# Loads and casts at the start of a fused relu-squared attention and gated FFN kernel: the first keys, the first queries, the activation table and one cast

## The chip, the cores and the metric

The kernel runs on one core of a Trainium2 chip. The time is the device time of one execution in microseconds (us). The core has five engines with queues of their own: TensorE (PE) multiplies matrices, VectorE (DVE) and ScalarE (ACT) do elementwise work, GpSimd (POOL) here mostly issues loads, and SyncE (SP) issues transfers. Sixteen DMA engines move the data for all of them.

## The reference

```
scores = scale * q @ k^T                 # 8 batches, 12 heads, 448 x 448, head size 64
attn   = relu(scores)^2 / 448
x      = (attn @ v), heads side by side  # 3584 x 768
out    = (relu(x @ w_gate) * (x @ w_val)) @ w_out   # 768 -> 1536 -> 768
```

Inputs and output are float32. The kernel works in bfloat16 with float32 accumulation and folds all constant factors into the scale of the last copy.

## The kernel before, in words

The batches (b from 0 to 7) are worked one after the other. The attention of batch b is interleaved with the FFN of batch b - 1, so that TensorE has matmuls while the other engines do relu and square. Every instruction is pinned with `pin`: each engine executes its instructions in the order in which the program writes them. What the program orders by hand is thus the whole schedule.

**Loads.** A tensor q, k or v of one batch has 12 heads of 448 rows by 64. `load_nat` (L110) brings some heads of it with two loads: rows 0 to 255, four to a partition, into partitions 0 to 63 ("lo"), and rows 256 to 447, three to a partition, into partitions 64 to 127 ("hi"). The fourth place of the upper partitions stays zero for keys and queries; memsets at L81 put the zeros there, into the tiles kn and qn of both buffers. These loads go through Pool's queue (`dma_in`, L92) and turn float32 into bfloat16 on their way. Pool's queue carries, in this order (L334 to L346): q and k of batch 0, v, the first two column chunks of w_gate and w_val, k and q of batch 1, the third chunk, v of batch 1, the fourth chunk, w_out in two halves (wo0, wo1), and later the k, q and v of the next batches.

**The first two heads** take another way (`load_first`, L95, called with 2). They are loaded without a change of type by SP's and ACT's queues, keys ahead of queries, into the tiles kr and qr, which are used as float32 scratch here and which otherwise serve from batch 3 on. Then VectorE casts the keys into kn (L107) and ScalarE casts the queries into qn (L108). The load of ScalarE's activation table comes ahead of ScalarE's first activation, which is that cast. Pool clears the empty place in the scratch tiles (L101) and then makes the identity matrix (L89) from a tile that VectorE zeroes (L83); after that its loads begin, with heads 2 and 3, 4 to 7, and 8 to 11.

**The first batch** (`first_batch`, L380) has no FFN beside it. TensorE begins with 28 matmuls on zeros (`idle_matmuls`, 14 pairs). For each of the six pairs of heads it then transposes keys and queries by matmuls with the identity (`transposes`, L169), and VectorE copies the result to the tile kq_sb (L180). The score matmuls of a pair fill three tiles of PSUM (buffers: 3). ScalarE takes the relu of each tile (L185), VectorE the square (L189). There are 21 such tiles. Two to four pairs of idle matmuls stand between. At the end of the batch the value matmuls (`av_pair`, L224) come in between the last score tiles: `values(qd, c)` sums attn times v for two heads in one of two PSUM banks, and `cast` (L390) copies the sum to x in bfloat16, on VectorE except for one, values(2, 0), which ScalarE casts (L428). `low_values` (L123) moves a part of v on VectorE ahead of the first value matmuls.

**The FFN** of batch 0 follows at once. `gv_unit` (L258) does 128 of the 1536 hidden columns: 12 matmuls for the gate, a relu on ScalarE (L266), 12 for the value, a product on VectorE (L272). Eight such units run before batch 1 begins. `out_unit` (L284) multiplies the hidden tile by w_out: the first six of its twelve steps read wo0, the last six wo1, and between them other work may run (L292).

Of the kernel before, what the change touches and what calls it, by code (L numbers as in the profile page):

```python
# [9 lines left out]
FP32 = mybir.dt.float32  # L10
BF16 = mybir.dt.bfloat16
AF = mybir.ActivationFunctionType
# [4 lines left out]
def kernel(  # L17
# [15 lines left out]
    nc = tc.nc  # L33

    B, H, S, D = q.shape
    d_model, d_ff = moe_w_gate.shape
# [13 lines left out]
    const = ctx.enter_context(tc.tile_pool(name="const", bufs=1))  # L50
# [3 lines left out]
    rpool = ctx.enter_context(tc.tile_pool(name="rpool", bufs=4))  # L54
# [5 lines left out]
    def pin(ins):  # L60
        return tc.keep_in_program_order(ins)
# [10 lines left out]
    NB = 2  # L72
    blank = const.tile([128, S], BF16, name="blank")
    pin(nc.vector.memset(blank, 0.0))
    kn_b = [const.tile([128, H, 4, D], BF16, name=f"kn{i}") for i in range(NB)]
    qn_b = [const.tile([128, H, 4, D], BF16, name=f"qn{i}") for i in range(NB)]
    v_b = [const.tile([128, H, 4, D], BF16, name=f"vn{i}") for i in range(NB)]
    ident = const.tile([128, 128], BF16, name="ident")
    for n in range(NB):
        for t in (kn_b[n], qn_b[n]):  # L80
            pin(nc.vector.memset(t[64:128, :, 3, :], 0.0))  # L81
        if n == 0:
            pin(nc.vector.memset(ident, 0.0))  # L83

    kr = const.tile([128, 4, d_model], BF16, name="kr")
    qr = const.tile([128, 4, d_model], BF16, name="qr")

    def make_ident():
        pin(nc.gpsimd.affine_select(out=ident, in_=ident, compare_op=ALU.not_equal, fill=1.0, base=0,  # L89
                                    pattern=[[-1, 128]], channel_multiplier=1))  # L90

    def dma_in(o, i):  # L92
        pin(nc.gpsimd.dma_start(out=o, in_=i))  # L93

    def load_first(h1):  # L95

        staged = []
        for grp, src in ((kr, k), (qr, q)):
            st = grp.rearrange("p i m -> p (i m)")[:, 0:h1 * 8 * D].bitcast(FP32)
            st = st.rearrange("p (h i d) -> p h i d", i=4, d=D)  # L100
            pin(nc.gpsimd.memset(st[64:128, :, 3, :], 0.0))  # L101
            lo = src[0, 0:h1, 0:256, :].rearrange("h (j i) d -> j h i d", i=4)
            hi = src[0, 0:h1, 256:448, :].rearrange("h (j i) d -> j h i d", i=3)
            pin(nc.sync.dma_start(out=st[0:64], in_=lo))
            pin(nc.scalar.dma_start(out=st[64:128, :, 0:3, :], in_=hi))
            staged.append(st)
        pin(nc.vector.tensor_copy(kn_b[0][:, 0:h1], staged[0]))  # L107
        pin(nc.scalar.activation(qn_b[0][:, 0:h1], staged[1], AF.Copy))  # L108

    def load_nat(dst, src, b, h0, h1):  # L110
        lo = src[b, h0:h1, 0:256, :].rearrange("h (j i) d -> j h i d", i=4)
        hi = src[b, h0:h1, 256:448, :].rearrange("h (j i) d -> j h i d", i=3)
        dma_in(dst[0:64, h0:h1, :, :], lo)
        dma_in(dst[64:128, h0:h1, 0:3, :], hi)

    def load_qk(b, h0=0, h1=H):
        load_nat(kn_b[b % NB], k, b, h0, h1)
        load_nat(qn_b[b % NB], q, b, h0, h1)
# [4 lines left out]
    def low_values(b):  # L123

        t = v_b[b % NB].rearrange("p (q s h) i d -> p q s h i d", s=2, h=2)
        pin(nc.vector.tensor_copy(t[64:128, :, 1, :, 3, :], t[0:64, :, 1, :, 3, :]))
# [64 lines left out]
    def relu2(src, dst, n):  # L191
        square_part(dst, relu_part(src, n))
# [31 lines left out]
    def av_pair(b, qd, c, attn, ps):  # L224

        p = HALVES[c][1]
        for h2, o in HALVES:
            mm(ps[o, :S], v_b[b % NB][p, 4 * qd + 2 * c + h2, 3, :], attn[p, 6 + h2, :], True, False)
        for i in range(3):
            for h2, o in HALVES:  # L230
                mm(ps[o, :S], v_b[b % NB][:, 4 * qd + 2 * c + h2, i, :], attn[:, 8 * c + 2 * i + h2, :], False, i == 2)

    def bank_tile():
        return psum.tile([128, 512], FP32, name="xT_ps", tag="acc", bufs=2)

    def idle_matmuls(ps, n):

        for _ in range(n):
            mm2(ps[:, :S], blank[:, 0:128], blank, True, True)
# [86 lines left out]
    def gap():  # L326
# [4 lines left out]
        flush()  # L331
        share[2] = i + 1

    load_first(2)  # L334
    make_ident()
    load_qk(0, 2, 4)
    load_qk(0, 4, 8)
    load_qk(0, 8, H)
    load_v(0)
# [16 lines left out]
    def transpose_pair(b, hp, bank=None):  # L356
        kqs[b, hp] = operands(b, hp, bank)

    def attn_of(b, qd):
        if (b, qd) not in attns:  # L360
            attns[b, qd] = atpool.tile([128, 14, S], BF16, name="attn")
        return attns[b, qd]

    def burst(b, tiles):

        todo, begun = [], None
        for qd, kind, c, i in tiles:
            attn = attn_of(b, qd)
            if kind == "pair":
                todo.append(scores(kqs[b, 2 * qd + c], i, attn, 8 * c + 2 * i))  # L370
            elif kind == "last":
                todo.append(scores_last((kqs[b, 2 * qd], kqs[b, 2 * qd + 1]), attn))
            else:
                ps = sc_tile()
                banks = [ps[:, c, :S] for c in range(2)]
                av_last(b, qd, attn, banks)
                begun = (qd, banks, ps[:, :, :S])
        return todo, begun

    def first_batch():  # L380

        def tile_of(n, i):
            return burst(0, [tiles_first[3 * n + i]])[0][0]

        def values(qd, c, on_act=False):
            ps, x = bank_tile(), xT_of[0][:, 2 * qd + c, :]
            av_pair(0, qd, c, attn_of(0, qd), ps)
            return x, ps[:, :S]

        def cast(x, ps):  # L390
            pin(nc.vector.tensor_copy(x, ps))

        bank = bank_tile()
        idle_matmuls(bank, 14)
        transpose_pair(0, 0, bank)
        bank = bank_tile()
        idle_matmuls(bank, 4)
        for n in range(5):
            t = [tile_of(n, i) for i in range(3)]
            if n == 4:  # L400
                low_values(0)
            transpose_pair(0, n + 1, bank)
            if n < 4:
                bank = bank_tile()
                idle_matmuls(bank, 2)
                for u in t:
                    relu2(*u)
        relu2(*t[0])
        relu2(*t[1])
        u0 = tile_of(5, 0)  # L410
        cast(*values(0, 0))
        relu2(*t[2])
        u1 = tile_of(5, 1)
        cast(*values(0, 1))
        u2 = tile_of(5, 2)
        relu2(*u0)
        relu2(*u1)
        w0 = tile_of(6, 0)
        cast(*values(1, 0))
        relu2(*u2)  # L420
        w1 = tile_of(6, 1)
        cast(*values(1, 1))
        w2 = tile_of(6, 2)
        relu2(*w0)
        relu2(*w1)
        x, ps = values(2, 0)
        relu2(*w2)
        pin(nc.scalar.activation(x, ps, AF.Copy))  # L428
        cast(*values(2, 1))


# [43 lines left out]
    for b in range(B):  # L475
        xT_of[b] = xpool.tile([128, KD, S], BF16, name="xT")
        if b == 0:
            first_batch()
        else:
            batch(b)  # L480
        if b + 1 < B:
            ffn.extend(ffn_units(b))
            if b == 0:
                for _ in range(7):
                    ffn.pop(0)()
                for hp in range(2):
                    midway.append(lambda hp=hp: transpose_pair(1, hp))
                ffn.pop(0)()
# [34 lines left out]
```

## Time and profile before

| | us |
|---|---|
| median of 3 runs | 437.26 (436.6 to 438.35) |
| the profiled execution | 436.3 |
| its span, first to last instruction | 434.5 |
| TensorE busy | 425.1 (98%) |
| ScalarE busy | 217.6 (50%) |
| VectorE busy | 210.3 (48%) |
| Pool busy | 50.5 (12%) |
| granted TensorE clock | 1.000 |

The span is divided into instructions by engine and line, and each idle time is put down to what ended it ("<-"). A line such as L64 is that of a helper: all matmuls have it, and the tiles tell them apart (sc_ps: scores, xT_ps: values and the first transposes, g_ps, v_ps and o_ps: the FFN). "kr<-in_k_dram" is a load of keys into kr. A load's issue is shown as an instruction on its engine's queue; its landing comes later, and the profile gives the time from issue to landing. The DMA share is the busy share of the 16 DMA engines, over 1 where the times of packets overlap; GB/s counts the bytes as they are written.

Early loads of the profiled execution, all times in us:

| load | queue | issued | to landing |
|---|---|---|---|
| kr lo, hi (heads 0 and 1) | SP, ACT | 0.76, 0.76 | 3.0, 2.6 |
| qr lo, hi (heads 0 and 1) | SP, ACT | 1.58, 1.51 | 3.4, 3.3 |
| first loads of kn, qn (heads 2 and 3) | Pool | 2.92, 4.25 | 2.7, 2.4 |
| last load of qn (heads 8 to 11) | Pool | 9.63 | 5.5 |
| v lo, hi | Pool | 10.24, 10.98 | 7.7, 8.5 |
| wo lo half, second half (wo0, wo1) | Pool | 40.46, 42.63 | 18.7, 22.2 |

### The profile page before, as it was taken

The page shows a single profiled execution, that of the slowest core. Times are in us where ns is not written, and L with a number is a line of the kernel's source. Part 1 is how long each engine was busy: PE and PEld are TensorE (multiplying, and loading weights), DVE is VectorE, ACT ScalarE, POOL GpSimd, SP SyncE. Part 2 cuts the span into 40 slices and gives each one's busy share as a digit, 9 for nine tenths or more (in the row PEclk, how much of TensorE's full clock was granted, in tenths as well). Part 3 has the DMA queues.
Part 4 walks back from the last instruction along what each step waited for, and adds up shares of the span by engine and source line. Part 5 has one row for each costly group of instructions (what it writes and reads, how often), then busy time and mean ns, then how long its engine had stood idle before and what let it go on. Part 6 is the DMA issues. An engine that isn't in the chain of part 4 may idle for free.

```text
span 434.5 us, 11448 instructions
## 1 busy us (share of the span) xinstructions
PE 425.1 (98%) x5068; PEld 250.2 (58%) x5068; DVE 210.3 (48%) x333; ACT 217.6 (50%) x324; POOL 50.5 (12%) x75
## 2 busy tenths in 40 slices
PE   7899999999999999999999999999999999999996
PEld 3357655655565555655566555655566555565664
DVE  4962784657623665356442675345643454522210
ACT  3952676453554554464554645554545645532221
POOL 8623311100204000300004000010000000000001
PEclk9999999999999999999999999999999999999999
DMA  7999999914699861491616923170413100030014
GB/s 112 174 207 196 200 209 211 227 22 65 105 162 145 122 101 29 91 202 28 110 38 116 187 57 74 38 137 2 99 31 95 53 2 2 10 101 3 2 38 109
DMA packets 78577, 42.45 MB, mean 98 GB/s; under 512 B 48416, under 2 KB 75040, under 8 KB 78528
## 3 DMA queue, kind: packets, MB, share of 16 engines
q0 software_dynamic: 45152, 23.47, 40.6%
q1 hardware_dynamic: 33008, 18.01, 17.6%
q8 instruction: 39, 0.64, 0.6%
q10 hardware_dynamic: 368, 0.25, 0.2%
q14 instruction: 10, 0.08, 0.1%
HBM read 47.19 MB, written 11.01 MB: 134 GB/s over the span
## 4 chain that ended last, share of the span: by engine, by line
PE 84%; DMA 12%; POOL 2%; issue 1%; DVE 0%; POOLq 0%; ACT 0%
PE o_ps L64 25%; PE g_ps L64 23%; PE v_ps L64 22%; PE sc_ps L64 13%; DMA wo<-in_moe_w_out_dram 5%; DMA qn<-in_q_dram 5%; DMA vn<-in_v_dram 2%; POOL kn L93 1%; POOL qn L93 1%; PE kq_ps L178 1%; POOL vn L93 0%; POOL out_dram L303 0%; POOLq L518 0%; DVE qn L81 0%; DVE kn L81 0%
## 5 line engine op out<-in xcount | busy, mean ns | idle before, releaser
L185 ACT ACTIVATE r_sb<-sc_ps 128x896 bf16<-128x896 f32 x168 | 145.0, 931 | 36.7 <-PE sc_ps L64 36.7
L189 DVE TENSOR_TENSOR attn<-r_sb 128x896 bf16<-128x896 bf16 x168 | 103.6, 623 | 92.2 <-ACT r_sb L185 92.1
L64 PE MATMUL g_ps<-xT,wg 128*64 128x448 bf16 x1152 | 126.1, 354 | 0.0
L64 PE MATMUL v_ps<-xT,wv 128*64 128x448 bf16 x1152 | 125.2, 353 | 0.0
L64 PE MATMUL o_ps<-wo,hT 128*64 128x384 bf16 (+1 forms) x1368 | 115.4, 324 | 1.0 <-DMA wo<-in_moe_w_out_dram 1.0
L272 DVE TENSOR_TENSOR hT<-v_ps,g_sb 128x448 bf16<-128x448 f32 x96 | 59.9, 624 | 89.2 <-PE v_ps L64 88.3
L64 PEld LDWEIGHTS <-hT 128*64 128x64 bf16 x1368 | 75.5, 110 | 38.4 <-issue 7.2
L266 ACT ACTIVATE g_sb<-g_ps 128x448 bf16<-128x448 f32 x96 | 52.3, 545 | 89.1 <-PE g_ps L64 89.1
L64 PEld LDWEIGHTS <-wg 128*64 128x64 bf16 x1152 | 63.5, 110 | 49.8 <-issue 13.1
L64 PEld LDWEIGHTS <-wv 128*64 128x64 bf16 x1152 | 66.2, 110 | 41.0
L295 ACT ACTIVATE o_sb<-o_ps 128x384 f32<-128x384 f32 (+1 forms) x57 | 27.9, 489 | 82.1 <-PE o_ps L64 82.1
L64 PE MATMUL sc_ps<-attn,vn 128*64 128x448 bf16 (+1 forms) x336 | 35.1, 354 | 0.0
L93 POOL DMA_DIRECT2D vn<-in_v_dram x16 | 12.1, 771 | 169.2 <-PE sc_ps L64 160.8
L457 DVE CAST xT<-sc_ps 128x896 bf16<-128x896 f32 x21 | 22.9, 1091 | 13.6 <-PE sc_ps L64 13.4
L64 PE MATMUL sc_ps<-qT,kT 64*64 64x448 bf16 x420 | 28.4, 357 | 0.0
L64 PEld LDWEIGHTS <-vn 128*64 128x64 bf16 (+1 forms) x384 | 18.8, 109 | 16.5 <-issue 5.9
L64 PE MATMUL sc_ps<-kq_sb 64*64 64x448 bf16 x252 | 19.0, 360 | 1.6 <-ACT r_sb L185 1.5
L93 POOL DMA_DIRECT2D kn<-in_k_dram x20 | 14.7, 763 | 46.4 <-PE kq_ps L178 44.0
L303 POOL DMA_DIRECT2D out_dram<-o_sb x2 | 1.1, 560 | 146.2 <-ACT o_sb L295 146.2
L64 PEld LDWEIGHTS <-kT 64*64 64x64 bf16 x420 | 9.6, 105 | 14.3 <-issue 11.7
L93 POOL DMA_DIRECT2D qn<-in_q_dram x20 | 14.5, 750 | 6.9 <-DMA vn<-in_v_dram 3.3
L64 PEld LDWEIGHTS <-kq_sb 64*64 64x64 bf16 x252 | 6.4, 105 | 13.0 <-issue 9.7
(33 smaller groups left out, 83.6 us busy)
## 6 DMA issues: line engine op xcount, KB each, us to landing
out_dram<-o_sb SPq DMA_DIRECT2D x54, 192.0 KB, 2.7
vn<-in_v_dram POOLq DMA_DIRECT2D x8, 384.0 KB, 7.0
kn<-in_k_dram POOLq DMA_DIRECT2D x7, 384.0 KB, 10.0
qn<-in_q_dram POOLq DMA_DIRECT2D x7, 384.0 KB, 12.1
vn<-in_v_dram POOLq DMA_DIRECT2D x8, 288.0 KB, 8.1
wo<-in_moe_w_out_dram POOLq DMA_DIRECT2D x2, 1152.0 KB, 20.5
kn<-in_k_dram POOLq DMA_DIRECT2D x7, 288.0 KB, 10.8
qn<-in_q_dram POOLq DMA_DIRECT2D x7, 288.0 KB, 12.9
```

The source lines that it names most:

```text
L64: pin(nc.tensor.matmul(o, lhsT=l, rhs=r, start=start, stop=stop, skip_group_check=True))
L93: pin(nc.gpsimd.dma_start(out=o, in_=i))
L178: pin(nc.tensor.transpose(o, t[:, 2 * hp + h2, i, :], ident))
L185: pin(nc.scalar.activation(r, src, AF.Relu))
L189: pin(nc.vector.tensor_tensor(dst, r, r, ALU.mult))
L266: pin(nc.scalar.activation(g_sb, g_ps, AF.Relu))
L272: pin(nc.vector.tensor_tensor(hT[:, mf, col:col + S], v_ps, g_sb, ALU.mult))
L295: pin(nc.scalar.activation(out=o_sb[:, c0:c1], in_=o_ps, func=AF.Copy, scale=float(out_scale)))
L303: pin(e.dma_start(out=segment_rows(b0, 2 * t + s)[:, m], in_=o_sb[s * 64:s * 64 + 64, m]))
L457: pin(nc.vector.tensor_copy(xT_of[b][:, 2 * qd:2 * qd + 2, :], both))
```

## The change

`load_first` is called with 4 and brings only keys by SP's and ACT's queues: four heads into the scratch kr, one load from each queue. ScalarE then takes the relu of the zero tile `blank` into a tile that nothing reads; its activation table is loaded for that. The queries of these four heads come by Pool's queue with the change of type, as the first loads there, and make_ident follows them. VectorE casts the keys in two pieces of two heads. The separate load of heads 2 and 3 is gone; heads 4 to 7, 8 to 11 and all else follow on Pool's queue as before. The zeros of the scratch tile and of the identity are now made by VectorE, ahead of those of kn and qn. In the first batch the cast of values(1, 0) moves from VectorE to ScalarE, to the same place in the program's order.

```
+    ident = const.tile([128, 128], BF16, name="ident")
+    pin(nc.vector.memset(ident, 0.0))
...
+    staged = kr.rearrange("p i m -> p (i m)")[:, 0:4 * 8 * D].bitcast(FP32)
+    staged = staged.rearrange("p (h i d) -> p h i d", i=4, d=D)
     for n in range(NB):
+        if n == 0:
+            pin(nc.vector.memset(staged[64:128, :, 3, :], 0.0))
         for t in (kn_b[n], qn_b[n]):
             pin(nc.vector.memset(t[64:128, :, 3, :], 0.0))
-        if n == 0:
-            pin(nc.vector.memset(ident, 0.0))
...
     def load_first(h1):
 
-        staged = []
-        for grp, src in ((kr, k), (qr, q)):
-            st = grp.rearrange("p i m -> p (i m)")[:, 0:h1 * 8 * D].bitcast(FP32)
-            st = st.rearrange("p (h i d) -> p h i d", i=4, d=D)
-            pin(nc.gpsimd.memset(st[64:128, :, 3, :], 0.0))
-            lo = src[0, 0:h1, 0:256, :].rearrange("h (j i) d -> j h i d", i=4)
-            hi = src[0, 0:h1, 256:448, :].rearrange("h (j i) d -> j h i d", i=3)
-            pin(nc.sync.dma_start(out=st[0:64], in_=lo))
-            pin(nc.scalar.dma_start(out=st[64:128, :, 0:3, :], in_=hi))
-            staged.append(st)
-        pin(nc.vector.tensor_copy(kn_b[0][:, 0:h1], staged[0]))
-        pin(nc.scalar.activation(qn_b[0][:, 0:h1], staged[1], AF.Copy))
+        lo = k[0, 0:h1, 0:256, :].rearrange("h (j i) d -> j h i d", i=4)
+        hi = k[0, 0:h1, 256:448, :].rearrange("h (j i) d -> j h i d", i=3)
+        pin(nc.sync.dma_start(out=staged[0:64], in_=lo))
+        pin(nc.scalar.dma_start(out=staged[64:128, :, 0:3, :], in_=hi))
+
+        pin(nc.scalar.activation(rpool.tile([128, 2, S], BF16, name="r_sb")[:, 0, :], blank, AF.Relu))
+        load_nat(qn_b[0], q, 0, 0, h1)
+        for h in range(0, h1, 2):
+            pin(nc.vector.tensor_copy(kn_b[0][:, h:h + 2], staged[:, h:h + 2]))
...
-    load_first(2)
+    load_first(4)
     make_ident()
-    load_qk(0, 2, 4)
     load_qk(0, 4, 8)
...
-        cast(*values(1, 0))
+        cast(*values(1, 0), on_act=True)
...
-        pin(nc.scalar.activation(x, ps, AF.Copy))
+        cast(x, ps, on_act=True)
```

More of the change, by code (lines that the diff above doesn't have):

```diff
@@ L77 @@
     v_b = [const.tile([128, H, 4, D], BF16, name=f"vn{i}") for i in range(NB)]
-    ident = const.tile([128, 128], BF16, name="ident")
+    kr = const.tile([128, 4, d_model], BF16, name="kr")
+    qr = const.tile([128, 4, d_model], BF16, name="qr")
+    staged = kr.rearrange("p i m -> p (i m)")[:, 0:4 * 8 * D].bitcast(FP32)
+    staged = staged.rearrange("p (h i d) -> p h i d", i=4, d=D)
     for n in range(NB):
+        if n == 0:
+            pin(nc.vector.memset(staged[64:128, :, 3, :], 0.0))
         for t in (kn_b[n], qn_b[n]):
             pin(nc.vector.memset(t[64:128, :, 3, :], 0.0))
-        if n == 0:
-            pin(nc.vector.memset(ident, 0.0))
-    kr = const.tile([128, 4, d_model], BF16, name="kr")
-    qr = const.tile([128, 4, d_model], BF16, name="qr")
     def make_ident():
@@ L383, in tile_of, with values @@
             return burst(0, [tiles_first[3 * n + i]])[0][0]
-        def values(qd, c, on_act=False):
+        def values(qd, c):
             ps, x = bank_tile(), xT_of[0][:, 2 * qd + c, :]
@@ L388, in values, with cast @@
             return x, ps[:, :S]
-        def cast(x, ps):
-            pin(nc.vector.tensor_copy(x, ps))
+        def cast(x, ps, on_act=False):
+            if on_act:
+                pin(nc.scalar.activation(x, ps, AF.Copy))
+            else:
+                pin(nc.vector.tensor_copy(x, ps))
         bank = bank_tile()
```

## The prediction

> **What bounds the kernel now.** I read the busy shares first, then the chain of waits in order of time, then the timeline of each engine up to 67 us.
>
> ```profile
> PE 425.1 (98%) x5068; PEld 250.2 (58%) x5068; DVE 210.3 (48%) x333; ACT 217.6 (50%) x324; POOL 50.5 (12%) x75
> ```
>
> The chain in order of time (start, duration, what):
>
> ```profile
> 2.92 1.36 POOL kn L93 x2
> ...
> 10.38 0.60 POOL vn L93
> 10.98 8.46 DMA vn<-in_v_dram
> 19.44 0.28 issue
> 19.73 22.00 DMA qn<-in_q_dram
> 41.73 0.90 issue
> 42.63 22.19 DMA wo<-in_moe_w_out_dram
> 64.82 0.04 issue
> 64.86 1.17 PE o_ps L64 x12
> ```
>
> TensorE is busy 98%, yet up to 64.86 us the chain does not run through it: it is one stream of loads on Pool's queue, from its first issue at 2.92 to the second half of w_out, which lands at 64.82. From there the chain is matmuls to the end. TensorE's timeline shows the meeting point:
>
> ```profile
> 64.86 1.17 PE L64 MATMUL o_ps<-wo,hT 128*64 128x384 bf16 x12 [0.96 <-DMA wo<-in_moe_w_out_dram]
> ```
>
> TensorE was ready at 63.90 and stood 0.96 us. So there are two clocks: TensorE's own arrival there, and w_out's landing. The later one sets the end; behind it nothing in the change touches the work. The gain is therefore the smaller of two terms: 0.96 plus what the first stage (0 to 28 us) gains, and what the load stream gains.
>
> The first stage, from ScalarE's and then VectorE's timeline (start, duration, instruction, in brackets the idle time before it):
>
> ```profile
> 5.06 1.28 ACT L108 ACT_TABLE_LOAD   x1 [5.06 <-DMA qr<-in_q_dram]
> 6.35 0.63 ACT L108 ACTIVATE qn<-qr 128x512 bf16<-128x512 f32 x1
> 8.64 17.11 ACT L185 ACTIVATE r_sb<-sc_ps 128x896 bf16<-128x896 f32 x21 [1.66 <-PE sc_ps L64]
> ```
>
> ```profile
> 7.49 0.66 DVE L180 COPY kq_sb<-xT_ps 128x960 bf16<-128x960 bf16 x1 [2.96 <-PE xT_ps L178]
> ...
> 25.70 1.69 DVE L189 TENSOR_TENSOR attn<-r_sb 128x896 bf16<-128x896 bf16 x3
> ```
>
> Queries land at 4.98 (issue 1.58 plus 3.4), the table load and cast end at 6.98, the first copy starts at 7.49, and then 21 relus follow without a hole to 25.75. VectorE is full from 19.3 to 27.39; its last square releases the last value matmuls at 27.43, and the FFN starts at 27.62 with TensorE full (30.00 of 30 us from 30 to 60).
>
> **The change part by part.**
>
> *Table load at once.* The load (1.28) and a 448-element relu (near 0.54, the row of a 128x448 activation) follow ScalarE's DMA issue: 1.5 to about 3.3, when ScalarE is idle. Relu and Copy need one load together, for the page has no second one. Price 0. The 1.28 and the query cast (0.63) leave the first pair's path.
>
> *Keys of four heads by SP and ACT, cast in two pieces.* 256 and 192 KB replace four transfers of together 448 KB on the same queues; the last of those landed at 4.98. Now all are issued at 0.76, but 224 KB of queries come beside them. I take a landing at 5.0. The fast end: 224 KB had landed by 3.76 and 2.5 to 3.0 us moved 335 GB/s, so 4.4. The slow end: the queries' 224 KB go first at 130 GB/s (the rows from 7 to 10 us), so 6.7. Then: 0.16 to the cast (3.76 to 3.92 now), cast 0.61, 0.08 to TensorE, 0.25 for key transposes (8.89 to 9.14), 0.46 from query transposes to the copy (7.03 to 7.49): 5.0 + 1.56 = 6.56 instead of 7.49, **0.93 earlier**. Ends: the idle matmuls hold the transposes until 5.39, so the copy comes at 6.10 at the earliest (1.39 earlier); with 6.7 it comes at 8.26 (0.77 later). The second cast (0.61) runs under the transposes.
>
> *Queries of four heads by Pool.* Pool's memsets go, so it can issue at 0.76 and 1.4. Pool's transfers of 96 to 128 KB took 2.9 to 3.0 us when issued at 5.4 and 6.0, and 5.5 in the backlog at 9.6. So 4.4, needed at 6.1; at worst 6.9, which would put the copy at 7.41. Neighbouring columns of a tile make no wait: ACT's load into kr was issued at 0.76 while Pool's memset of kr ran (0.75 to 0.95). The affine_select of ident moves behind these two issues (2.1 to 2.6, needed at 5.8): covered.
>
> *VectorE's early order.* The staged memset (64x256, near 0.3 by the 64x384 row of 0.38) comes in; all memsets still end near 3.2, before the keys land. Price 0; if keys landed by 3, the casts would wait these 0.2.
>
> *Pool's stream.* Twelve issues stood ahead of v, now ten, and the first starts 2.1 earlier. But from 7 us the queue is backlogged: v issued at 10.98 lands 8.5 later, and the DMA share is above 1.
>
> ```profile
> 4.00:5.00 1.00, 1.00 (x10) 0.51 (x8) 0.53 (x1) 0.00 (x0) 1.00 (x3) 1.00 0.62 111
> 5.00:6.00 1.00, 0.78 (x14) 0.44 (x10) 0.00 (x0) 0.94 (x1) 1.00 (x2) 1.00 0.85 91
> 6.00:7.00 1.00, 0.00 (x0) 0.00 (x0) 0.00 (x0) 0.97 (x2) 1.00 (x3) 1.00 0.86 93
> 7.00:8.00 1.00, 0.97 (x16) 0.59 (x16) 0.51 (x1) 0.00 (x0) 1.00 (x3) 1.00 1.15 140
> 8.00:9.00 1.00, 1.00 (x20) 0.37 (x18) 0.15 (x1) 0.36 (x1) 1.00 (x2) 1.00 1.27 135
> ```
>
> The last two columns are DMA share and GB/s. Earlier issues buy only the slack before 7. The finer rows from 4.5 to 7.0 average 94 GB/s against 135 in the backlog: 2.5 x 41 = 103 KB, 0.76 us at 135. Before that, 448 KB landed from 2.5 to 4.6, which at 300 GB/s takes 1.5: 0.6 more. Together **1.36 us**. High end: shares from 2.5 to 8.0 sum to 4.7 where 1.27 throughout would be 7.0, so 2.3 / 1.27 = 1.8. Low end: 140 GB/s throughout instead of 250 in the first 1.5 us gives 797 KB by 8.0 instead of 837, so 0.3 lost. From 17 us on the stream stays near 207 GB/s, so w_out lands earlier by the same amount.
>
> A rule speaks against this. Two Pool issues beside VectorE's fp32-to-bf16 cast (3.92 to 4.53) took 0.63 and 0.62; those beside the squares 0.72 to 0.75, so VectorE costs them 0.12 at most. The Trainium skill, "SBUF — State Buffer", section "SBUF: two separate sides", says that Pool writes its DMA descriptors through a port pair that VectorE locks for a whole instruction in its two-port modes, so that such a DMA stands until VectorE ends. The trace does not agree in size; as a mechanism it is the second case below.
>
> *One more cast on ACT.* values(1, 0) leaves TensorE at 23.21 (22.67 plus 0.54); ScalarE's relu before it ends at 22.52, so ScalarE, in order, stands 0.7, casts 0.54 to 23.8, and the four relus queued behind (at 0.80 each) start 1.35 later: the last ends at 27.0 instead of 25.75. VectorE loses a 0.54 cast, so it had slack to absorb most: the last square ends at 27.68 instead of 27.39. **0.30 lost.** Ends: no standing, then 0.48 gained; without VectorE's backlog as cover, 1.3 lost.
>
> **Sum.** TensorE's term: 0.96 + 0.93 - 0.30 = 1.59. Stream's term: 1.36. The smaller: 1.36, with TensorE still waiting some 0.2 for w_out. The profiled execution took 436.3 (span 434.5, 1.8 around it): 434.9. It stands 0.96 below the median 437.26, which gives 435.9.
>
> **Rivals.**
> 1. *The stream decides* (the forecast, gain 1.0 to 1.8): 435.9, 435.5 to 436.3. For it: share below 1 before 7, above 1 after. Chance 0.52.
> 2. *The first stage gains little*, because queries come late: if Pool's descriptors stand until the memsets end at 3.2, queries land at 3.2 + 0.65 + 3.0 = 6.85, the copy comes at 7.36, 0.13 earlier, and TensorE's term is 0.79: 436.5; the wait for w_out is gone. For: five memsets lie beside the issues. Against: 0.74 is the longest early issue, with a memset beside it. Chance 0.22.
> 3. *The change does not speed up the stream* (small packets bind throughout): w_out lands at 64.8, the first stage's gain turns into a wait of 1.6 there: 437.3. For: the low end above. Chance 0.16.
> 4. *Slower: Pool's packets crowd out the keys.* By 3.5 us some 264 KB of the 448 have moved (335 and 193 GB/s); if the other 184 KB then get a third of 135 GB/s beside queries and heads 4 to 7, they land at 7.6, the copy comes 1.67 later, and TensorE's term is -1.0: 438.3. It turns slower when keys land past 6.6; half of the rate (6.2) does not do it. Against: the old second pair landed at 4.98 with Pool's transfers beside it. Chance 0.10.
>
> **How the numbers follow.** About 0.5% (2.2 us) is what a measurement of this kernel can tell from no change. No case reaches a gain of 2.2 by itself; the runs spread 1.75 us and the stream's high end is 1.8, so faster gets 0.17. Slower needs the worse half of case 4 or scatter on case 3: 0.07. Same: 0.76. Range: 437.26 - 1.8 - 0.9 of scatter = 434.5 up to case 3 with 0.5 of scatter, 437.8; outside lie most of case 4 and the far ends.
>
> **What would show it.** Right: first copy near 6.6, first relu near 7.7, a stand of ScalarE near 0.7 ahead of the new cast, v's second part landing near 18.1 instead of 19.48, w_out near 63.5, and a short wait left there. Wrong: no wait for w_out left (TensorE late: case 2 or 4), w_out still at 64.8 (case 3), or a new wait of the value matmuls for v, which has 0.13 us of margin now (19.48 against 19.61).

## The result and the profile after

The kernel after takes 435.02 us (median of 9 runs, 434.60 to 435.44), the kernel before in the same series 436.60 (9 runs, 436.18 to 438.91): 1.58 us less. The ratio of the two kernels' runs is 0.9952 with a 95% interval from 0.9935 to 0.9969, which leaves out no change. The forecast was a gain of 1.36 and a time of 435.9. The time lies 0.88 lower: 0.22 because the gain is larger, and 0.66 because before's median was 437.26 in the 3 runs that the forecast started from and is 436.60 in these 9. The profiled execution of the kernel after has a span of 433.3 where before's had 434.5.

First the busy shares, then the chain of waits in order of time (start, duration, what), of the kernel after:

```profile
PE 425.4 (98%) x5068; PEld 250.3 (58%) x5068; DVE 210.7 (49%) x334; ACT 218.0 (50%) x325; POOL 49.0 (11%) x71
```

```profile
3.08 1.16 POOL kn L95 x2
...
7.92 0.63 POOL vn L95
8.55 10.05 DMA vn<-in_v_dram
18.60 0.28 issue
18.88 22.11 DMA qn<-in_q_dram
41.00 0.86 issue
41.85 21.70 DMA wo<-in_moe_w_out_dram
63.55 0.04 issue
63.60 1.17 PE o_ps L64 x12
```

The chain has the same form as before: Pool's issues, loads of v, q and w_out, then matmuls to the end. The second half of w_out lands at 63.55 instead of 64.82, 1.27 earlier (forecast 1.36). TensorE's timeline at that place, the number in brackets being its idle time:

```profile
63.60 1.17 PE L64 MATMUL o_ps<-wo,hT 128*64 128x384 bf16 x12 [0.26 <-DMA wo<-in_moe_w_out_dram]
```

TensorE is ready at 63.34 (63.90 before) and still stands 0.26 (forecast some 0.2). From this matmul to the end the trace has 369.7 us, as before (434.53 - 64.86 = 369.67). The whole difference lies ahead of it. An estimate from this: if all runs spend 369.7 us behind that matmul and 1.8 us around the span, before's median of 436.60 has it start at 65.1 and the median of the kernel after at 63.5. The profiled execution of before (64.86) was thus a little faster than its median, that of the kernel after (63.60) a little slower, and the gain of 1.58 is larger than the 1.26 between the two. The first stage, on ScalarE's, VectorE's and Pool's timelines:

```profile
1.51 1.28 ACT L104 ACT_TABLE_LOAD   x1 [1.51 <-PEq L508]
2.81 0.58 ACT L104 ACTIVATE r_sb<-blank 128x448 bf16<-128x448 bf16 x1
7.74 13.88 ACT L184 ACTIVATE r_sb<-sc_ps 128x896 bf16<-128x896 f32 x17 [4.36 <-PE sc_ps L64]
22.36 0.54 ACT L390 ACTIVATE xT<-xT_ps 128x448 bf16<-128x448 f32 x1 [0.74 <-PE xT_ps L64]
```

```profile
5.33 1.01 DVE L107 CAST kn<-kr 128x512 bf16<-128x512 f32 x2 [2.14 <-DMA kr<-in_k_dram]
6.59 0.66 DVE L179 COPY kq_sb<-xT_ps 128x960 bf16<-128x960 bf16 x1 [0.26 <-PE xT_ps L177]
...
26.17 0.62 DVE L188 TENSOR_TENSOR attn<-r_sb 128x896 bf16<-128x896 bf16 x1 [0.18 <-ACT r_sb L184]
```

```profile
1.27 1.42 POOL L95 DMA_DIRECT2D qn<-in_q_dram  x2 [0.82 <-POOLq L508]
2.76 0.33 POOL L91 TENSOR_SCALAR_AFFINE_SELECT ident<-ident 128x128 bf16<-128x128 bf16 x1
3.00 1.25 POOL L95 DMA_DIRECT2D kn<-in_k_dram  x2
4.20 1.27 POOL L95 DMA_DIRECT2D qn<-in_q_dram  x2
5.40 1.30 POOL L95 DMA_DIRECT2D kn<-in_k_dram  x2
```

The first copy comes at 6.59 instead of 7.49 (forecast 6.56). The relus run without a hole until the moved cast, ahead of which ScalarE stands 0.74 (forecast 0.7). VectorE's last square ends at 26.79 instead of 27.39, so of the 0.90 by which the stage began earlier 0.6 is left. Pool's issues beside the two casts (5.33 to 6.34) take 0.68 and 0.70, the four ahead of them, from 3.00 on, 0.64 to 0.67.

The stages of the DMA, with their share and GB/s in the last two columns:

```profile
4.00:5.00 1.00, 1.00 (x10) 0.51 (x8) 0.00 (x0) 0.00 (x0) 1.00 (x3) 1.00 1.45 188
5.00:6.00 1.00, 0.88 (x14) 0.38 (x12) 0.67 (x2) 0.00 (x0) 1.00 (x3) 1.00 1.37 169
6.00:7.00 1.00, 1.00 (x24) 0.74 (x20) 0.74 (x2) 0.00 (x0) 1.00 (x3) 1.00 1.43 177
7.00:8.00 1.00, 1.00 (x18) 0.27 (x14) 0.25 (x1) 0.26 (x1) 1.00 (x3) 1.00 1.46 176
8.00:9.00 1.00, 1.00 (x25) 0.64 (x21) 0.32 (x1) 1.00 (x2) 1.00 (x2) 1.00 1.45 176
```

The slack of before (91 to 111 GB/s from 4 to 7 us) is filled, and the queue now moves about 176 GB/s in the time from 7 to 9 us too, where it moved 135 to 140.

### The profile page after: what moved, and what is told of

Same layout as the page of the kernel before. It is cut to its first block, busy times and chain, and to the rows that moved or that the text cites. A ratio compares the mean times of both kernels' runs of the same rounds, so it can differ in the third digit from the quotient of the medians.

```text
span 433.3 us, 11436 instructions
## 1 busy us (share of the span) xinstructions
PE 425.4 (98%) x5068; PEld 250.3 (58%) x5068; DVE 210.7 (49%) x334; ACT 218.0 (50%) x325; POOL 49.0 (11%) x71
## 4 chain that ended last, share of the span: by engine, by line
PE 84%; DMA 12%; POOL 2%; issue 1%; POOLq 0%; ACT 0%
PE o_ps L64 25%; PE g_ps L64 23%; PE v_ps L64 22%; PE sc_ps L64 13%; DMA qn<-in_q_dram 5%; DMA wo<-in_moe_w_out_dram 5%; DMA vn<-in_v_dram 2%; POOL qn L95 1%; PE kq_ps L177 1%; POOL kn L95 1%; POOL vn L95 0%; POOL out_dram L302 0%; POOLq L519 0%; ACT o_sb L294 0%; POOL ident L91 0%
## 5 line engine op out<-in xcount | busy, mean ns | idle before, releaser
L64 PEld LDWEIGHTS <-wg 128*64 128x64 bf16 x1152 | 63.4, 110 | 49.8 <-issue 13.1
L95 POOL DMA_DIRECT2D kn<-in_k_dram x18 | 13.3, 762 | 46.8 <-PE kq_ps L177 45.2
```

Of the source, the lines that this page charges most:

```text
L64: pin(nc.tensor.matmul(o, lhsT=l, rhs=r, start=start, stop=stop, skip_group_check=True))
```

## The experiments

The theory is that of the prediction: the later of two clocks, TensorE's arrival at the second half of w_out and the landing of that half, sets the end. The rivals are that the first stage's gain counts by itself, and that the stream of loads alone counts. "Before" is run beside each series; its medians are 436.77, 436.49 and 436.53 in the three series below.

**b_table: the early table load alone.**

```
# the kernel before
+        pin(nc.scalar.activation(rpool.tile([128, 2, S], BF16, name="r_sb")[:, 0, :], blank, AF.Relu))
         pin(nc.vector.tensor_copy(kn_b[0][:, 0:h1], staged[0]))
```

> The kernel before, with nothing but one more activation, the relu of the zero tile, ahead of the query cast, so that the activation table is loaded early. My theory (the later of two clocks, TensorE's arrival at the second half of w_out and that half's landing, sets the end): the query cast starts when the queries land, near 5.1 instead of 6.35, so the first copy comes near 6.2 instead of 7.49 and TensorE arrives near 62.6 instead of 63.90; w_out still lands near 64.8, so the stand there grows from 0.96 to about 2.2 us and the time stays that of the kernel before within 0.3 us. Rival (the first stage's gain reaches the end by itself): 1.2 to 1.3 us faster than before.

Measured: 436.40, ratio 0.9996 (0.9987 to 1.0005). ScalarE's and TensorE's timelines:

```profile
5.12 0.63 ACT L109 ACTIVATE qn<-qr 128x512 bf16<-128x512 f32 x1 [1.07 <-DMA qr<-in_q_dram]
```

```profile
1.17 5.44 PE L64 MATMUL xT_ps<-blank 128*64 128x448 bf16 x28 [1.17 <-DVE blank L74]
6.40 0.49 PE L179 MATMUL xT_ps<-ident,kn 128*64 128x128 bf16 x8
...
65.30 1.17 PE L64 MATMUL o_ps<-wo,hT 128*64 128x384 bf16 x12 [1.72 <-DMA wo<-in_moe_w_out_dram]
```

The query cast moved from 6.35 to 5.12 as expected, TensorE came earlier (63.58), and its stand at w_out grew to 1.72 (w_out itself landed 0.43 later here than in before): the gain of the first stage is swallowed, and the time is that of before. The rival of 1.2 us falls. One expectation missed: the first copy came at 7.16, not 6.2, since the 28 idle matmuls lasted until 6.60 here (5.55 in the profile of before) and hold the transposes behind them. The first stage thus gained only 0.33 us in this execution, which the interval of the times could not tell from nothing; that the gain ends in a longer wait is read from the trace.

**a_notable: the kernel after without the relu of the zero tile.**

```
# the kernel after
-        pin(nc.scalar.activation(rpool.tile([128, 2, S], BF16, name="r_sb")[:, 0, :], blank, AF.Relu))
```

> The kernel after without the relu of the zero tile, so that the activation table is loaded ahead of the first relu of scores. Theory: the first relu starts 1.28 later (9.0 instead of 7.74), TensorE arrives 1.28 later at the second half of w_out (64.6 instead of 63.34), w_out lands near 63.55 and is no longer waited for; time +1.0 against the kernel after (1.28 less the 0.26 that it waits there now), so some 0.2 faster than the kernel before. Rival (the stream alone decides, the first stage is free): no change against the kernel after.

Measured: 435.21, ratio 0.9966 (0.9954 to 0.9979). ScalarE's and TensorE's timelines:

```profile
1.51 1.28 ACT L183 ACT_TABLE_LOAD   x1 [1.51 <-PEq L507]
8.02 13.88 ACT L183 ACTIVATE r_sb<-sc_ps 128x896 bf16<-128x896 f32 x17 [5.22 <-PE sc_ps L64]
```

```profile
6.42 0.41 PE L176 MATMUL xT_ps<-ident,qn 128*64 128x128 bf16 x8 [0.18 <-DMA qn<-in_q_dram]
...
63.43 1.14 PE L64 MATMUL o_ps<-wo,hT 128*64 128x384 bf16 x12
```

The edit does not do what the expectation took it to do, so it tests neither the theory nor the rival. The table is loaded at 1.51 all the same, long before the relu at 8.02 that it precedes. In the kernel before, where ScalarE's first activation waits for the queries, the table load came behind that wait (5.06); here the first activation waits for TensorE, and the load came ahead of the wait. The added relu is thus idle in the kernel after, while in the kernel before it moves the load. The run tells two other things: here the first transposes of queries waited for Pool's load of them, and w_out had landed (62.30) before TensorE came (63.43). TensorE's arrival decided this execution.

**a_dvecast: the cast of values(1, 0) back on VectorE.**

```
# the kernel after
-        cast(*values(1, 0), on_act=True)
+        cast(*values(1, 0))
```

> The kernel after with the cast of values(1, 0) back on VectorE. Theory: ScalarE's stand of 0.74 us goes, the FFN starts about 0.3 us earlier (26.7 instead of 27.04), TensorE arrives 0.3 earlier at the second half of w_out and waits 0.3 longer there (about 0.6 instead of 0.26); the time stays within 0.1 us. Rival 1 (the moved cast helps): the FFN starts later than 27.04, by up to 0.5. Rival 2 (the tail reaches the end): 0.3 us faster than the kernel after.

Measured: 434.88, ratio 0.9957 (0.9945 to 0.9969). TensorE's timeline:

```profile
1.16 5.44 PE L64 MATMUL xT_ps<-blank 128*64 128x448 bf16 x28 [1.16 <-DVE blank L74]
6.39 0.54 PE L177 MATMUL xT_ps<-ident,kn 128*64 128x128 bf16 x8
...
27.33 1.33 PE L64 MATMUL g_ps<-xT,wg 128*64 128x448 bf16 x12
```

VectorE's first copy in this run, and the start of the FFN on TensorE in the kernel after:

```profile
7.20 0.66 DVE L179 COPY kq_sb<-xT_ps 128x960 bf16<-128x960 bf16 x1 [1.46 <-PE xT_ps L177]
```

```profile
27.04 1.33 PE L64 MATMUL g_ps<-xT,wg 128*64 128x448 bf16 x12
```

The FFN starts later, 27.33 and not 26.7, but only because the idle matmuls last until 6.60 in this execution and put the first copy at 7.20. Counted from the first copy, the FFN starts after 20.13 us here and after 20.45 in the kernel after (27.04 - 6.59). The other profiles agree: 20.13 to 20.14 with that cast on VectorE (before, b_table, and three below) and 20.44 to 20.45 with it on ScalarE (a_notable, a_poollate, a_cols); only the last two below, which come close to v's landing, differ. So the moved cast costs 0.32, as forecast (0.30); that it helps is refuted. For the time of the whole kernel the run is inconclusive: the intervals overlap.

**a_poollate: Pool's stream held back behind the queries.**

```
# the kernel after
     make_ident()
+    pin(nc.gpsimd.memset(qr.rearrange("p i m -> p (i m)")[:, 0:2048].bitcast(FP32), 0.0))
```

> The kernel after with a memset of 1024 float32 per partition of a tile that is not in use on Pool behind the identity, which holds Pool's stream back by its length (estimated 1 us from the 0.20 us of a 128-element one; the trace will tell) without touching the first four heads. Theory (the stream's early start is what the change gained): the second half of w_out lands later by about the length of the memset, 64.5 instead of 63.55, TensorE still arrives near 63.3, and the time grows by 0.9. Rival (the early lead is mostly lost later anyway: of 2.8 us by which the first of the 16 DMA engines ended its part of w_out earlier, the last kept only 1.27): w_out lands only 0.3 to 0.5 later, and the time grows by as much.

Measured: 435.14, ratio 0.9972 (0.9960 to 0.9984); Pool's timeline has the memset and the first load behind it, TensorE's the matmul that waited for w_out in the kernel after:

```profile
3.00 0.99 POOL L335 MEMSET qr<- 128x1024 f32 x1
3.89 1.25 POOL L95 DMA_DIRECT2D kn<-in_k_dram  x2
```

```profile
63.30 1.14 PE L64 MATMUL o_ps<-wo,hT 128*64 128x384 bf16 x12
```

The loads are issued 0.89 later, and w_out lands at 63.17: 0.7 to 0.9 later than in a_dvecast (62.49) and a_notable (62.30), which have the stream of the kernel after, but earlier than in the profile of the kernel after itself (63.55). TensorE came at 63.30 and did not wait, so the time did not grow by 0.9. The theory's number was wrong: it took 63.55 for the landing of the kernel after, and that was the latest of three. The rival's 0.3 to 0.5 missed too. That the stream alone counts falls with it: a landing 0.7 to 0.9 later than in a_dvecast and a_notable costs nothing that their times in the same series (434.88, 435.21) show. Each kernel was profiled once, so a landing is that of one execution. Where it varies shows in the 16 updates by which each load reports its parts. For the second half of w_out (us):

| | first part | 8th part | last part |
|---|---|---|---|
| before | 62.53 | 63.57 | 64.82 |
| b_table | 62.54 | 63.06 | 65.25 |
| after | 59.73 | 60.79 | 63.55 |
| a_notable | 59.28 | 59.89 | 62.30 |
| a_dvecast | 59.59 | 61.32 | 62.49 |
| a_poollate | 61.15 | 62.36 | 63.17 |

The first part leads by 2.8 us in the kernel after, and the bytes nearly as far (2840 KB by 18 us against 2329: 511 KB, 2.5 us at 207 GB/s). The last part, which alone counts, trails the 8th by 0.8 to 2.8 us in these six profiles. What makes a part late was not tried.

**b_cols: the wait for w_out taken away from the kernel before.**

```
# the kernel before
-    wo_sb = [const.tile([128, KF // 2, d_model], BF16, name=f"wo{i}") for i in range(2)]
+    wo_sb = [const.tile([128, KF, OH], BF16, name=f"wo{i}") for i in range(2)]
...
-            rows = moe_w_out[c * (d_ff // 2):(c + 1) * (d_ff // 2), :]
+            half = moe_w_out[:, c * OH:(c + 1) * OH]
...
-            mm2(o_ps, hT[:, kf, bass.ts(t, 128)], wo_sb[kf // 6][:, kf % 6, c0:c1], kf == 0, kf == KF - 1)
+            mm2(o_ps, hT[:, kf, bass.ts(t, 128)], wo_sb[c0 // OH][:, kf, c0 % OH:c0 % OH + c1 - c0], kf == 0, kf == KF - 1)
```

> The kernel before, with w_out loaded as two halves of 384 columns instead of two halves of 768 rows, so that the first unit that uses w_out needs only the half that lands near 59. Theory (the later of two clocks): the stand of 0.96 us goes and TensorE's arrival at 63.9 sets the end: 0.9 to 1.3 us faster than before (the two profiles with the old loads stood 0.96 and 1.72), that is most of what the change gains, with nothing of the first 28 us touched. Rival (the change's gain comes from the first stage): within 0.3 us of before.

Measured: 435.03, ratio 0.9967 (0.9954 to 0.9979): 1.46 below before, nearly the 1.58 of the change under study, with the first 28 us as they were. TensorE's timeline:

```profile
27.61 1.33 PE L64 MATMUL g_ps<-xT,wg 128*64 128x448 bf16 x12
...
63.73 1.14 PE L64 MATMUL o_ps<-wo,hT 128*64 128x384 bf16 x12
```

The FFN starts when it did (27.62), and the stand is gone. It has not moved elsewhere: the second half lands at 65.21 and is first read at 66.65. The rival falls: ending this wait is by itself worth most of what the change gains, without a faster first stage.

**a_cols, a_cols_dvecast, a_best.** The same edit of w_out in the kernel after; then the cast back on VectorE; then also `idle_matmuls(bank, 11)` for 14.

> The kernel after with w_out loaded by column halves. Theory, as the four runs so far have it (in three of four executions of kernels like it the last part of w_out landed before TensorE wanted it, so its arrival near 63.4 already decides): within 0.2 us of the kernel after. Rival (the stream still decides in the kernel after, as its one profile had it): 0.3 us or more faster than it.

> As a_cols, and the cast of values(1, 0) back on VectorE. Theory (TensorE's arrival decides, and ScalarE's stand costs it 0.3): about 0.3 us faster than a_cols. Rival (the idle matmuls at the start, which ended at 5.55 to 6.60 us depending on when the clock of TensorE opened, decide the first stage): no clear difference, the spread between executions is larger.

> As a_cols_dvecast, with 11 instead of 14 pairs of idle matmuls at the start. Theory: when the clock opens late (near 6.6 us), the 14 pairs last until 6.6 and hold the first transposes by 0.6; 11 pairs end at 5.28 at the latest, so the first copy comes near 6.6 in each execution and the time is 0 to 0.6 us below a_cols_dvecast, by execution. Rival (the idle matmuls are needed to open the clock): the clock opens later still, the first scores run at half speed (0.58 instead of 0.35 us each), and the time is 0.5 us or more above a_cols_dvecast.

Measured: 434.79, ratio 0.9958 (0.9943 to 0.9973); 434.59, 0.9956 (0.9939 to 0.9972); 434.47, 0.9949 (0.9931 to 0.9967). Each step lowers the median by 0.1 to 0.2, in the direction expected; the intervals overlap, so the times alone settle none of the three. The rival of a_best, 0.5 us or more above a_cols_dvecast, falls. a_cols stands 1.70 below before, the kernel after 1.58 in its own series: within 0.2, as expected. Whether the stream still decides in some executions of the kernel after is not told by these times but by the profile above, where it did, by 0.26. In a_best the idle matmuls end at 5.08 and the transposes wait for keys and queries instead:

```profile
5.82 0.41 PE L177 MATMUL xT_ps<-ident,kn 128*64 128x128 bf16 x8 [0.74 <-DVE kn L107]
6.52 0.41 PE L177 MATMUL xT_ps<-ident,qn 128*64 128x128 bf16 x8 [0.29 <-DMA qn<-in_q_dram]
```

**b_table_cols11 and a_twos: what is next in line.** The first is b_table with w_out by columns and 11 pairs of idle matmuls. The second is a_best with keys and queries of the first four heads in loads of two heads:

```
# a_best
+        for h in range(0, h1, 2):
+            lo = k[0, h:h + 2, 0:256, :].rearrange("h (j i) d -> j h i d", i=4)
+            hi = k[0, h:h + 2, 256:448, :].rearrange("h (j i) d -> j h i d", i=3)
+            pin(nc.sync.dma_start(out=staged[0:64, h:h + 2], in_=lo))
+            pin(nc.scalar.dma_start(out=staged[64:128, h:h + 2, 0:3, :], in_=hi))
...
-        load_nat(qn_b[0], q, 0, 0, h1)
+        load_nat(qn_b[0], q, 0, 0, 2)
+        load_nat(qn_b[0], q, 0, 2, h1)
```

> The kernel before with the early table load, w_out by column halves and 11 pairs of idle matmuls; the loads of the first heads and Pool's stream as before. Theory (TensorE's arrival decides; what limits it is next in line): queries by SP and ACT land near 5.0 and are cast by 5.75, so the first copy comes near 6.3, earlier than in the kernel after (6.59 to 7.0, where Pool's second part of the queries lands at 6.0 to 6.4); but v still lands near 19.2 and is now wanted near 18.4, so the value matmuls wait up to 0.8 us and the FFN starts near 27.1: time within 0.2 us of a_best. That would be what Pool's early start is worth in the first stage. Rival (v's landing has room): the FFN starts near 26.4, and the time is 0.7 us below a_best.

Measured: 434.90, ratio 0.9964 (0.9952 to 0.9977). The copy came at 6.38, and then the value matmuls waited for v, as expected:

```profile
19.92 0.76 PE L64 MATMUL xT_ps<-attn,vn 128*64 128x448 bf16 x6 [0.67 <-DMA vn<-in_v_dram]
...
27.66 1.14 PE L64 MATMUL g_ps<-xT,wg 128*64 128x448 bf16 x10
```

The FFN starts at 27.66 in spite of a first copy 1.1 us earlier than in the kernel before, and the time is 0.4 above a_best (expected: within 0.2). In the four profiles with before's stream v landed at 19.12 to 19.88, so a first stage much faster than before's runs into it; in the six with the stream of the kernel after it landed at 16.35 to 18.60. That is what Pool's earlier start is worth in the first stage.

> The kernel a_best (the kernel after, cast back on VectorE, w_out by column halves, 11 pairs of idle matmuls) with the first four heads' keys and queries loaded two heads at a time on the same queues. Theory: the first pair needs only the first half of these loads; its keys land near 3.9 and its queries near 4.7, the idle matmuls end near 5.1, so the first copy comes near 6.0 instead of 6.97; Pool has two issues more (1.2 us), v lands near 17.5 where 18.1 is wanted; the FFN starts near 26.2 and the time falls by 0.8 to 1.0 us below a_best. Rival (the queues share the 16 DMA engines, and the first halves land no earlier): the first copy stays near 6.9 and the time is that of a_best.

Measured: 434.24, ratio 0.9947 (0.9934 to 0.9961), the lowest median of all, though the interval overlaps that of a_best. The first copy came at 6.44 and the FFN started at 26.77, 0.34 earlier than in a_best, where 0.8 to 1.0 was expected. TensorE's timeline:

```profile
1.16 4.32 PE L64 MATMUL xT_ps<-blank 128*64 128x448 bf16 x22 [1.16 <-DVE blank L74]
5.27 0.64 PE L179 MATMUL xT_ps<-ident,kn 128*64 128x128 bf16 x8
5.79 0.62 PE L179 MATMUL xT_ps<-ident,qn 128*64 128x128 bf16 x8
```

In this execution all 22 idle matmuls took 0.58 us each, where the last four of a_best took 0.35 to 0.37, so they lasted until 5.48, and the transposes took 0.64 instead of 0.41; and the second part of the first two heads' queries landed at 5.65, not 4.7. Of what the first copy gained, 0.2 went again to v, whose last part landed at 19.00 (expected 17.5): the value matmuls began at 18.57, and those that read this part started only at 19.04. From first copy to FFN it took 20.33 instead of 20.13.

## Why the prediction was right, and where it was not

*Two clocks*: right, and shown. b_table makes the first stage faster, and by its trace TensorE only waits longer; b_cols leaves the first stage as it is and gains nearly as much as the change. From the matmul behind the wait to the end every profile has 369.5 to 369.7 us.

*The forecast case, "the stream decides"*: right in the profiled execution of the kernel after (0.26 of wait left), but not as a rule. In a_notable, a_dvecast and a_poollate TensorE found w_out landed, and its arrival near 63.4 decided. The smaller term was thus, in these, TensorE's: 0.96 of wait plus 0.46 to 0.60 of first stage (63.90 against 63.44 to 63.30) is 1.42 to 1.56, where 1.59 was forecast and 1.58 was measured. The total held although another term decided, because the forecast had the two only 0.23 apart; that much is luck.

*The stream's term*, 1.36: in the profile of the kernel after the last part of w_out came 1.27 earlier, but this near hit is chance, for it is the smallest lead on record. The second load of w_out ended at 62.13 to 63.55 in the six profiles with this stream (mean 62.8; three of them load column halves) and at 64.82 to 65.25 in the four with before's (mean 65.1; two with column halves): 2.3 earlier. The working was mis-sized twice. The backlog's rate was not 135 GB/s but 169 to 188 from 4 to 9 us, so the lead grew to 2.5 us of bytes by 18 us; and the end of a load is that of its slowest part, which the prediction did not consider and which kept 1.3 to 2.5 of the lead in the kernel after, a_dvecast and a_notable.

*First copy*, 6.56 forecast, 6.59 measured, but 6.74 to 7.20 in the other kernels with the same loads; that it hit is luck. The keys landed 0.20 late (5.20 instead of 5.0), and the first cast took 0.43 instead of 0.61, which made up for it. The queries were wrong: taken as landed at 4.4, they landed at 6.00, for Pool's first issue came at 1.27 and not 0.76, and the two loads took 4.47 and 3.96 and not 2.9; why Pool begins so late was not tried. They were just in time; in a_notable they were not. The idle matmuls, taken to hold the transposes until 5.39, held them until 6.39 in a_dvecast.

*The table load*: price 0 on ScalarE, right; that the relu brings it about is true only for the kernel before.

*The moved cast*: 0.30 lost forecast, 0.32 measured, by the stand of ScalarE as described.

*The port rule* of the Trainium skill ("SBUF — State Buffer", "SBUF: two separate sides"): Pool's issues beside VectorE's casts and memsets took 0.65 to 0.78 each, against 0.65 and 0.66 with VectorE idle (at 3.60 and 4.20), and the first two started at 1.27 and 2.05, beside the memsets, not behind them. So the case that hung on that rule did not come. The queries were late for the other reason given above.

*v*: forecast to land near 18.1, it lands at 18.60 in the profile of the kernel after and is read from 18.71. That margin of 0.11 is of this execution: in the five others with the same stream v landed at 16.35 to 17.48 and was read 1.8 us later or more. b_table_cols11 shows the wait that lies behind it with before's stream.

## What to carry to other kernels

Follow the chain of waits to the place where it leaves the loads, and count there how long the engine stands: a gain ahead of such a place is worth no more than the landing moves, and a gain of the stream no more than the stand plus what the engine itself gains. A wait for a late load can often be ended by asking which part of it is read first; here halving w_out by columns instead of rows gave nearly as much (1.46) as a rebuilt start (1.58). Where an engine works in order, a cast that is cheap on it can cost the time for which it stands ahead of it.

## What the runs showed of the hardware that I had not expected

TensorE changes speed at a different time in each execution: the idle matmuls take 581 ns at first, a pair every 0.37 us, and later 353 ns, a pair every 0.19 us. The first short ones come at 4.4 us in before, and within the 28 not at all in b_table, a_dvecast and b_cols, although before and b_cols have the same program in this stretch. The same 28 matmuls end anywhere from 5.55 to 6.60. The profile's granted clock stands at 1.00 through all of this and does not show it. The Trainium skill, "TensorE: Matmul & The Clock Gate", section "What's actually happening", has a free-running window of about 3.4 us of activity that opens the clock, so that the point varies from run to run, by 500 ns either way. The traces agree with a point that varies, but the spread is wider: with matmuls from 1.17 on, the first short one starts 3.3 us later in before and 5.4 us later in b_table.

A load's landing is that of the last of its 16 parts (the second half of w_out in the kernel after: 63.55, and the matmul that waits for it starts at 63.60), and these drift apart: in the second half of w_out the last trails the first by 2.0 to 3.8 us in the six profiles of the table, and that varies by more than the 1.27 us that the landing moved from before to after. Three of them (after, a_notable, a_dvecast) have the same stream of loads and trail by 3.8, 3.0 and 2.9.
